# Attention and two mixture-of-experts layers on one core: row tiles of 112 and 128 partitions, a routing step and a count one block on, transposes in other PSUM banks

## The chip, the cores and the metric

The kernel runs on one core of a Trainium2 chip. The metric is device time in microseconds (us); the figure for the kernel before is the median of its timed runs. The profile is of one further execution, taken by the hardware profiler.

## The reference

Three parts follow one another, all in float32.

1. Attention as a recurrence over 768 positions, for 2 batches of 8 heads of width 48: `state = alpha * state + k v^T`, `y = q state`. The result is laid out as x with 1536 rows (tokens) of 384.
2. Layer one of experts. Each token goes to the one of 8 experts with the largest of `x @ w_gate`; an expert computes `relu(x @ w1) @ w2` (384 to 1024 to 384), weighted by the softmax's value.
3. Layer two of experts. Logits get noise scaled by `log(1 + exp(x @ w_noise))`; the best two of 8 experts are taken for each token, and their outputs, weighted by a softmax over the two, are added.

The rows of a token therefore travel: attention, one expert, then two experts, then a sum in the output.

## The kernel before, in words

**Stages.** Up to about 90 us the kernel computes attention, the first routing and the first weight splits. Then come 16 jobs in a fixed order, `jobs` (L439): layer one's experts 0 to 7 (n = 0 to 7), then layer two's (n = 8 to 15; the code calls job 8 `E`). Each job has a room of C rows: 240 in layer one; in layer two 304 for expert 0, 432 for expert 1, and for the other six, sorted by their number of rows, 432, 412, 400, 396, 384 and 384 (`CAPS`, L28). Rows travel through two stores in HBM, `xs1` and `xs2`, to which they are scattered by an indirect DMA on GpSimd's queue (`indirect`, L153) and from which the next expert loads them.

**A job.** The loop at L1131 writes out 8 hidden blocks and then 8 second blocks. A hidden block (`hidden`, L636) is nine matmuls (each operand is split into a high and a low part in the fast float32 format, hence three products for each of three slices of 384). A second block (`second`, L655) is nine more. Between the blocks the loop emits, in program order for every engine:

- `split(n + 1, q, eng)` and `split_rest()` (L498, L513): the next job's weights are cut into high and low, the high part by ScalarE (L510) and the low part by a subtraction on VectorE or GpSimd (L511), which is put off to the next `split_rest`.
- `step(prev, ...)`: one or more pieces of the job before's tail, a generator that yields between its pieces. In layer one that is `job_route2` (L788) with `route2` (L678), which computes the logits of layer two, picks two experts, ranks the rows by matmuls with a triangle of ones (L768 to L771, "the rank matmuls"), works out slots (L774 to L779), scatters the rows to `xs2` (four indirect DMAs, L780 to L782) and adds to the counts `acc2` (L784, L785; "the last piece" is L774 to L785). In layer two it is `finish2` (L836).
- `load_x`, `split_x` (L560, L584): the next job's rows are loaded and turned over.

**Where the pieces fall.** `STEPS` (L58) has three strings of 16 digits: for layer one's jobs, for job 8 and for those after. Digit i says how many pieces are done after block i (0 to 7 the hidden blocks, 8 to 15 the second ones). In the string of layer one the rank matmuls fall after second block 2 and the last piece after second block 3.

**From layer one to layer two.** Job 8 needs rows from all of layer one. `load_x(8)` is emitted in job 7 after hidden block 3 on GpSimd's queue (L1139, L566) and reads the rows that the tails of experts 0 to 5 scattered; the rows of experts 6 and 7 that go to layer two's expert 0 are put behind and handled late (`load_late`, `late_tokens`, L864 to L914). Job 7 turns x of job 8 over in second blocks 5, 6 and 7 (three PE transposes for each slice of 128, L603, then L607 on ScalarE and L608 on VectorE). In job 8 `order(2, acc2)` (L459, matmul L462) counts rows for each expert and sorts six of them; from block 3 on, the loads for job 10 use its result.

**Row tiles.** `dims` (L541) gives for each job the number of row tiles and the partitions of each. `tiles` (L552) gives the slices. In layer two a tile has 108 partitions, except in the last two jobs (128). The tiles set how rows lie in SBUF after `load_x` (row tile t, partition p is row t * p_count + p), how many rows are read, the PE transposes, and the rows of each scatter into the output.

**PSUM.** Three tags of banks: `ph` (3 buffers), `py` (3), `pm` (2) (L99 to L106). `route2` holds one `pm` buffer (`pa`) from its first piece to its last. `finish2` of job 8 is emitted by the string `AFTER` (L62) after job 8's second blocks, mixed with the late rows' work (`l`) and the turning of x for job 9 (`x`); its output transposes (L857 to L859) take `pm` buffers, and `weigh` (L824) scales a tile with ScalarE (even tiles, L827) or VectorE (odd ones, L829) and scatters it to the output.

Of the kernel before, what the change touches and what calls it, by code (L numbers as in the profile page):

```python
# [16 lines left out]
N, DM, E, F = B * S, H * D, 8, 1024  # L17
# [5 lines left out]
C2, T2 = 432, 4  # L23
# [3 lines left out]
NF2 = 2  # L27
# [27 lines left out]
LX = 9  # L55
SP = 7
WG = 8
STEPS = ("0111122111110000", "1232210200000000", "0112111010100000")  # L58
ENGS = ("VGGGGGGGGVVVVVGV", "GGGGGGGGGGGVGGVG")
XS = ("135", "024", "567")  # L60
LATE_F = 3
# [5 lines left out]
def body(tc, ap, cap, dbg=False, stop=False):  # L67
    nc = tc.nc
    V, A, G, PE = nc.vector, nc.scalar, nc.gpsimd, nc.tensor
    with ExitStack() as ctx:  # L70
# [5 lines left out]
        def sb(shape, tag, bufs, dt=F32):  # L76
            cnt[0] += 1
            return pool.tile(list(shape), dt, name=f"{tag}_{cnt[0]}", tag=tag, bufs=bufs)
# [16 lines left out]
        def ps(tag, bufs):  # L95
            cnt[0] += 1
            return psum.tile([128, 512], F32, name=f"{tag}_{cnt[0]}", tag=tag, bufs=bufs)

        def ph():  # L99
            return ps("ph", 3)  # L100
# [4 lines left out]
        def pm():  # L105
            return ps("pm", 2)  # L106
# [4 lines left out]
        xs2 = dram.tile([SPARE + 2 * E * C1 + 256, RW], F32, name="xs2")  # L111
# [86 lines left out]
        def zero_rows(store, e, n, r, k=128):  # L198

            nc.sync.dma_start(store[:E * R].rearrange("(e r) d -> r e d", e=E)[r:r + k, e:e + n],  # L200
                              zt[0][:k, None, :RW].to_broadcast([k, n, RW]))
# [9 lines left out]
        def zero_xs2():  # L211
            zero_rows(xs2, 0, 1, LOW3)
            zero_rows(xs2, 0, E, LOW2)
            zero_rows(xs2, NF2, E - NF2, C2, -C2 % 32)

        def zero_out(i):
            nc.sync.dma_start(out[i * 512:(i + 1) * 512].rearrange("(p k) d -> p (k d)", p=128), zt[0][:, :4 * DM])
# [225 lines left out]
        def place(n):  # L443

            layer, e = jobs[n]
            return e - NF2 if layer == 2 and e >= NF2 else None
# [66 lines left out]
        def split_rest():  # L513
            now, rest[:] = list(rest), []
            for o in now:
                o()
# [24 lines left out]
        def dims(n):  # L541

            layer, e = jobs[n]
            c, t = (C1, T1) if layer == 1 else (C0, T0) if e == 0 else (C2, T2)
            p = C2 // T2 if layer == 2 else c // t
            if place(n) is not None:
                c = CAPS[place(n)]
                if c <= 384:
                    t, p = 3, 128
            return t, p, c  # L550

        def tiles(n):  # L552
            nt_, p, c = dims(n)
            return [(t, slice(t * p, min(c, t * p + p)), min(c - t * p, p)) for t in range(nt_)]
# [245 lines left out]
        def tokens_of(g):  # L800

            p, t = g.shape[0], g.shape[1]
            ix, iz = sm([128, T2], "ix", I32, 3)[:p, :t], sm([128, T2], "iz")[:p, :t]
            V.tensor_scalar(iz, g[:, :, GT], 0.0, None, op0=ALU.is_equal)
            V.tensor_tensor(iz, iz, tro[:p, :t], op=ALU.mult)
            V.scalar_tensor_tensor(iz, g[:, :, TK], 0.0, iz, op0=ALU.max, op1=ALU.add)
            V.tensor_scalar(ix, iz, float(N + 128 * T2 - 1), None, op0=ALU.min)
            return ix
# [15 lines left out]
        def weigh(sc, t, y, ix, ysc, group):  # L824
            r = y.shape[0]
            if t % 2 == 0:
                A.activation(ysc[:r, t, :], y, AF.Copy, scale=sc[:r, t, :])  # L827
            else:
                V.tensor_scalar(ysc[:r, t, :], y, sc[:r, t, :], None, op0=ALU.mult)  # L829
            indirect(out, ix[:r, t:t + 1], ysc[:r, t, :], group, ALU.add)  # L830

        def by_row(n):

            return range(3) if place(n) is not None and dims(n)[2] == 384 else None

        def finish2(n):  # L836
            nt_, p, c = dims(n)
            yp = yps.pop(n)
            if by_row(n):
                ix, ysc, group = tokens_of(xg[n]), sb([p, nt_, DM], "b6", 5), []  # L840
                yield
                for t in range(nt_):
                    weigh(own[n], t, yp[t][:, :DM], ix, ysc, group)
                    yield
                return
            yT = sb([128, ND, c], "b6", 5)
            for d in range(ND):
                if d == 1:
                    V.tensor_copy(yT[:, d, :], yp[d][:, :c])
                else:  # L850
                    A.activation(yT[:, d, :], yp[d][:, :c], AF.Copy)  # L851
            ix = tokens_of(xg[n])
            ysc = sb([p, nt_, DM], "b6", 5)
            yield
            group = []
            for t, sl, r in tiles(n):
                bp = pm()  # L857
                for d in range(ND):
                    PE.transpose(bp[:r, d * 128:(d + 1) * 128], yT[:, d, sl], ident)  # L859
                weigh(own[n], t, bp[:r, :DM], ix, ysc, group)  # L860
                yield
# [261 lines left out]
        def step(it, n=1):  # L1123
            for _ in range(n if it is not None else 0):
                next(it, None)
# [5 lines left out]
        for n, (layer, e) in enumerate(jobs):  # L1131
            steps = STEPS[0 if n < E else 1 if n == E else 2]
            eng = [G if x == "G" else V for x in ENGS[layer - 1]]
            step(prev)
            for f in range(NF):
                hidden(n, f)
                split_rest()
                step(prev, int(steps[f]))
                if f == (3 if n == E - 1 else 0) and n not in (E, 2 * E - 1):  # L1139
                    load_x(n + 1, nc.gpsimd)  # L1140
                if f == 4 and layer == 2:
                    own_weight(n)
                if f % 4 == 2:
                    raw(n + 1, 2 + f // 4)
                if n != E + 1:
                    split(n + 1, f, eng[f])
                else:
                    split(n, 8 + f, eng[f])
                    if f >= 4:
                        split_rest()  # L1150
                        split(n + 1, f - 4, eng[f])
            if n < 2 * E - 1:
                for f in range(NF):
                    if n == E and f == LATE_F:
                        for _ in prev:
                            pass
                        g = load_late(nc.sync)
                        load_x(n + 1, nc.sync)
                        raw(n + 2, 0)
                        it = late_tokens(n, g)  # L1160
                    xs_ = XS[2 if n == E - 1 else layer - 1]
                    if n != E and str(f) in xs_:
                        split_x(n + 1, xs_.index(str(f)))
                    second(n, f, by_row(n))
                    split_rest()
                    step(prev, int(steps[8 + f]))
                    if n == E and f == 0:
                        order(2, acc2)
                    if f % 4 == 2 and (n, f) != (E, 2):
                        raw(n + 2, f // 4)  # L1170
                    if n < 4 and f == 5:
                        zero_out(n)
                    if n != E:
                        split(n + 1, 8 + f, eng[8 + f])
                    if n == E + 1 and f < 4:
                        split_rest()
                        split(n + 1, 4 + f, eng[8 + f])
                if n == E - NL:

                    cp = pm()  # L1180
                    PE.matmul(cp[:, 0:1], ones, acc2[:, 0:1], start=True, stop=True)
                    V.tensor_scalar(eb3[:, 0:1], cp[:, 0:1], -1.0, float(C0), op0=ALU.mult, op1=ALU.add)
                    V.tensor_scalar(eb3[:, 0:1], eb3[:, 0:1], 0.0, None, op0=ALU.max)
                prev = job_route2(n) if layer == 1 else finish2(n)
                d = 0
                for o in AFTER if n == E else ():
                    if o == "x":
                        split_x(n + 1, d)
                        d += 1
                    else:  # L1190
                        step(prev if o == "f" else it)
            else:
                nt_, p, c = dims(n)
                ix = tokens_of(xg[n])
                ysc = sb([p, nt_, DM], "b6", 5)
                group = []
                it = beyond()
                for t in range(nt_):
                    if t:
                        step(it)  # L1200
                    for f in range(NF):
                        second(n, f, (t,))
                    weigh(own[n], t, yps[n][t][:tiles(n)[t][2], :DM], ix, ysc, group)
# [217 lines left out]
```

## Time and profile before

| What | Value |
|---|---|
| Median of 3 timed runs | 482.88 us (481.26 to 483.62) |
| The profiled execution's own time | 478.29 us |
| Its span, first to last instruction | 476.7 us |
| Mean granted TensorE clock, share of 2.4 GHz | 0.996 |
| TensorE matmul busy | 460.9 us, 97% |
| VectorE, ScalarE, GpSimd busy | 318.9, 263.4, 318.9 us |
| DMA, mean over the span | 193 GB/s |

How to read it: busy time of TensorE counts pipelined matmuls, so the idle time between them is the better measure of what other engines cost it. The timeline view gives for an engine each instruction's start (us from the span's start), its duration, the engine, the line and the operation, and in square brackets how long the engine had been idle before it and what ended that. A group in it merges neighbours of one line. Line numbers are the kernel's. VectorE is DVE, ScalarE ACT, GpSimd POOL, SyncE's DMA queue SPq.

### The profile page before, as it was taken

What the parts mean: (1) busy time and instruction counts of PE and PEld (TensorE: products, weight loads), DVE (VectorE), ACT (ScalarE), POOL (GpSimd) and SP (SyncE); (2) the same over time, 40 slices, a digit from 0 to 9 for tenths busy, and PEclk for the clock granted to TensorE, in tenths of its full rate; (3) what the DMA queues carried; (4) which work ended last, traced back from release to release, by engine and by line L of the source; (5) the groups of instructions that cost most, each with busy time, mean ns of one, the idle gap of its engine ahead of it and who ended that gap; (6) DMA issues with size and microseconds to landing.
All of it is one profiled execution on the core that took longest, in us unless ns stands there. A gap on an engine that the chain in (4) does not pass through costs nothing.

```text
span 476.7 us, 9770 instructions
## 1 busy us (share of the span) xinstructions
PE 460.9 (97%) x3431; PEld 433.8 (91%) x3434; DVE 318.9 (67%) x902; ACT 263.4 (55%) x683; POOL 318.9 (67%) x400
## 2 busy tenths in 40 slices
PE   8999999999999999999899899999999999999993
PEld 4588888899999999999899799999999999999992
DVE  8999988557887887888973425935364472837440
ACT  3477787467667677676561356444553545455310
POOL 3435596576778778776865249798694958869312
PEclk9999999999999999999999999999999999999998
DMA  8984863589999978768443953778483955551232
GB/s 293 408 248 160 301 236 132 202 285 320 325 272 256 293 237 261 213 220 251 162 157 105 285 131 101 182 172 210 124 180 112 212 153 119 120 160 24 26 42 41
DMA packets 64421, 92.13 MB, mean 193 GB/s; under 512 B 22301, under 2 KB 47134, under 8 KB 64362
## 3 DMA queue, kind: packets, MB, share of 16 engines
q1 hardware_dynamic: 56202, 77.22, 53.0%
q0 software_dynamic: 8160, 14.19, 13.9%
q8 instruction: 29, 0.48, 0.4%
q14 instruction: 30, 0.25, 0.2%
HBM read 70.76 MB, written 20.63 MB: 192 GB/s over the span
## 4 chain that ended last, share of the span: by engine, by line
PE 77%; DVE 12%; issue 4%; ACT 2%; DMA 2%; POOL 2%; POOLq 0%; DVEq 0%; ACTq 0%
PE py L673 31%; PE ph L644 20%; PE ph L647 10%; DVE h L650 2%; PE pm L367 2%; PE ph L291 2%; PE pm L859 2%; DVE s L511 2%; PE pm L701 2%; PE py L338 1%; PE py L344 1%; PE py L318 1%; DVE s L238 1%; PE py L911 1%; PE ph L886 1%
## 5 line engine op out<-in xcount | busy, mean ns | idle before, releaser
L511 POOL TENSOR_TENSOR s<-s,s 128x384 fp32r<-128x384 f32 x175 | 183.1, 1231 | 38.7 <-issue 21.5
L673 PE MATMUL py<-h,s 128*128 128x240 f32 (+5 forms) x1008 | 147.3, 305 | 0.0
L673 PEld LDWEIGHTS py<-h,s 128*128 128x128 f32 x1008 | 142.6, 189 | 1.2
L644 PE MATMUL ph<-x,s 128*128 128x240 f32 (+6 forms) x768 | 135.6, 312 | 0.8 <-ACT x L630 0.6
L510 ACT ACTIVATE s<-s 128x384 fp32r<-128x384 f32 x256 | 124.7, 516 | 1.5 <-DMA s<-w 1.5
L644 PEld LDWEIGHTS ph<-x,s 128*128 128x128 f32 x768 | 115.6, 189 | 2.8 <-ACT x L630 1.0
L650 DVE SCALAR_TENSOR_TENSOR h<-ph,h 128x240 fp32r<-128x240 f32 (+6 forms) x128 | 60.8, 483 | 68.3 <-ACT h L649 67.3
L649 ACT ACTIVATE h<-ph 128x240 fp32r<-128x240 f32 (+6 forms) x128 | 55.4, 433 | 60.2 <-PE ph L647 59.9
L511 DVE TENSOR_TENSOR s<-s,s 128x384 fp32r<-128x384 f32 x81 | 79.8, 989 | 1.7 <-ACT s L510 1.4
L647 PE MATMUL ph<-x,s 128*128 128x240 f32 (+6 forms) x384 | 76.7, 308 | 0.0
L157 POOL DMA_INDIRECT out<-b,m_ix x29 | 46.6, 1607 | 37.9 <-ACT b L827 16.9
L647 PEld LDWEIGHTS ph<-x,s 128*128 128x128 f32 x384 | 61.2, 189 | 0.4
L157 POOL DMA_INDIRECT xs<-b,m_si x32 | 33.4, 1045 | 21.0 <-DVE pm L784 15.9
L300 POOL TENSOR_SCALAR_AFFINE_SELECT h<-h 128x512 f32<-128x512 f32 x24 | 22.9, 977 | 26.6 <-ACT h L299 26.6
L595 ACT ACTIVATE x<-pm 128x240 fp32r<-128x240 f32 (+5 forms) x39 | 16.9, 433 | 41.6 <-DVE pm L592 38.2
L673 PE MATMUL py<-s,h 128*128 128x384 f32 x144 | 25.9, 339 | 0.0
L673 PEld LDWEIGHTS py<-s,h 128*128 128x128 f32 x144 | 25.2, 188 | 0.0
L596 DVE TENSOR_TENSOR x<-pm,x 128x240 fp32r<-128x240 f32 (+5 forms) x39 | 18.7, 480 | 9.1 <-ACT x L595 9.1
L851 ACT ACTIVATE b<-py 128x432 f32<-128x432 f32 (+4 forms) x12 | 5.9, 501 | 27.3 <-PE py L673 27.3
L592 DVE STREAM_TRANSPOSE pm<-b 128x256 f32<-128x256 f32 (+3 forms) x39 | 20.5, 526 | 0.0
L238 DVE TENSOR_TENSOR s<-s,s 112x256 f32<-112x256 f32 (+2 forms) x24 | 19.3, 824 | 0.6
L155 POOL MEMSET spacer<- 1x1 f32 x74 | 19.6, 264 | 0.1
(244 smaller groups left out, 556.5 us busy)
## 6 DMA issues: line engine op xcount, KB each, us to landing
s<-w SPq DMA_DIRECT2D x38, 768.0 KB, 6.7
s<-w_1b SPq DMA_DIRECT2D x14, 768.0 KB, 7.3
s<-w_2b SPq DMA_DIRECT2D x12, 768.0 KB, 6.1
xs<-s SPq DMA_DIRECT2D x2, 1576.0 KB, 7.2
out<-s SPq DMA_DIRECT2D x4, 768.0 KB, 8.1
b<-xs SPq DMA_DIRECT2D x28, 96.0 KB, 5.7
b<-xs SPq DMA_DIRECT2D x12, 156.0 KB, 6.0
s<-as SPq DMA_DIRECT2D x2, 780.5 KB, 6.6
```

What stands on the lines that cost most here:

```text
L155: G.memset(spacer, 0.0)
L157: st = G.indirect_dma_start(out=dst, out_offset=bass.IndirectOffsetOnAxis(ap=ix, axis=0), in_=src, in_offset=None, **kw)
L238: eng.tensor_tensor(o, src[:, h].rearrange("r (s j) -> r s j", j=64), x[:, h].rearrange("r (s j) -> r s j", j=64), op=ALU.mult)
L300: G.affine_select(a_, a_, pattern=[[0, 4], [1, 128]], compare_op=ALU.is_ge, fill=0.0, base=0, channel_multiplier=-1)
L510: A.activation(hi[sl], t[sl], AF.Copy)
L511: rest.append(lambda: (eng or V).tensor_tensor(lo[sl], t[sl], hi[sl].bitcast(F32), op=ALU.subtract))
L592: V.transpose(y.rearrange("p (t j) -> p t j", j=32), x)
L644: PE.matmul(p, w, x[:, d, :], start=(k == 0), stop=False)
L647: PE.matmul(p, w1_of(n, f, d)[0], xl[:, d, :], start=False, stop=(d == ND - 1))
L649: A.activation(hh, p, AF.Relu)
L650: V.scalar_tensor_tensor(hl, p, 0.0, hh.bitcast(F32), op0=ALU.max, op1=ALU.subtract)
L673: PE.matmul(out_, l, r, start=(f == 0 and k == 0), stop=(f == NF - 1 and k == 2))
```

## The change

Five edits. The row tiles of layer two get 128 partitions for expert 0 (tiles of 128, 128 and 48 rows in place of 108, 108 and 88) and 112 for the others with four tiles (for 432 rows 112, 112, 112 and 96); jobs with three tiles of 128 stay. Row loads take whole tiles, so expert 0's load reads 384 rows in place of 324, and those with four tiles 448 in place of 432. The zeroing of store rows 432 to 447 takes in expert 1 as well. In layer one the rank matmuls move from after second block 2 to after block 3 and the last piece from after block 3 to after block 4. In job 8 `order` moves from after second block 0 to after block 1. The output transposes of job 8 take `ph` buffers in place of `pm`.

```diff
-STEPS = ("0111122111110000", "1232210200000000", "0112111010100000")
+STEPS = ("0111122111011000", "1232210200000000", "0112111010100000")
...
-            zero_rows(xs2, NF2, E - NF2, C2, -C2 % 32)
+            zero_rows(xs2, 1, E - 1, C2, -C2 % 32)
...
             c, t = (C1, T1) if layer == 1 else (C0, T0) if e == 0 else (C2, T2)
-            p = C2 // T2 if layer == 2 else c // t
+            p = c // t if layer == 1 else 128 if e == 0 else 112
...
             for t, sl, r in tiles(n):
-                bp = pm()
+                bp = ph() if n == E else pm()
                 for d in range(ND):
                     PE.transpose(bp[:r, d * 128:(d + 1) * 128], yT[:, d, sl], ident)
...
                     step(prev, int(steps[8 + f]))
-                    if n == E and f == 0:
+                    if n == E and f == 1:
                         order(2, acc2)
```

## Rows read from the trace of the kernel before

**Rows 1.** The page's first lines: span, busy time and share of each engine.
```profile
span 476.7 us, 9770 instructions
PE 460.9 (97%) x3431; PEld 433.8 (91%) x3434; DVE 318.9 (67%) x902; ACT 263.4 (55%) x683; POOL 318.9 (67%) x400
```

**Rows 2.** Busy time by stage: stretch and length, engines' busy, clock, DMA share, GB/s.
```profile
88.00:237.60 149.60, 147.06 (x1303) 145.44 (x1304) 120.90 (x445) 99.89 (x279) 109.07 (x140) 1.00 0.82 250
237.60:275.00 37.40, 35.24 (x237) 32.53 (x237) 18.76 (x73) 13.59 (x36) 18.42 (x25) 1.00 0.65 190
275.00:464.00 189.00, 188.96 (x1049) 185.25 (x1047) 99.98 (x178) 92.56 (x203) 139.21 (x155) 1.00 0.56 128
```

**Rows 3.** Timeline of TensorE, the instructions before which it was idle, and L886.
```profile
139.20 0.17 PE L768 MATMUL pm<-accs,tri 120*120 120x8 bf16 x1 [0.23 <-DVE m_wt L763]
...
233.12 0.45 PE L603 MATMUL pm<-iw,b 108*128 108x108 f32 x3 [1.05 <-DMA b<-xs]
...
234.99 0.45 PE L603 MATMUL pm<-iw,b 108*128 108x108 f32 x3 [0.37 <-DVE accs L785]
...
252.25 0.18 PE L462 MATMUL pm<-accs,ones 128*128 128x8 bf16 x1 [0.40 <-DVE accs L785]
...
261.52 0.52 PE L874 MATMUL pm<-iw,h 128*128 128x128 f32 x3 [0.20 <-DMA h<-xs]
...
263.09 0.54 PE L859 MATMUL pm<-iw,b 128*108 128x128 f32 x3 [0.72 <-ACT b L827]
263.38 4.40 PE L886 MATMUL ph<-s,x 128*128 128x512 f32 x18
```

**Rows 4.** The transposes' matmuls by line: duration ns min/median/max, first and last start, forms.
```profile
L603 PE MATMUL pm<-iw,b x9: 241/256/283, 233.1 to 236.5; 108*128 108x108 f32 x6, 88*128 88x88 f32 x3
...
L859 PE MATMUL pm<-iw,b x69: 270/272/318, 261.9 to 423.9; 128*108 128x128 f32 x57, 128*88 128x128 f32 x6, 128*76 128x128 f32 x3, 128*72 128x128 f32 x3
```

**Rows 5.** Timeline of VectorE around the last piece in job 6.
```profile
212.73 0.53 DVE L511 TENSOR_TENSOR s<-s,s 128x384 fp32r<-128x384 f32 x1
213.19 0.16 DVE L774 TENSOR_TENSOR pm<-pm,eb 120x16 f32<-120x16 f32 x1
...
214.25 0.17 DVE L785 CAST accs<-pm 120x8 bf16<-120x8 f32 x1
214.34 0.40 DVE L596 TENSOR_TENSOR x<-pm,x 128x240 fp32r<-128x240 f32 x1
214.65 0.55 DVE L511 TENSOR_TENSOR s<-s,s 128x384 fp32r<-128x384 f32 x1
```

**Rows 6.** Timeline of GpSimd from job 6's scatters to job 8's row load.
```profile
214.31 1.05 POOL L157 DMA_INDIRECT xs<-b,m_si  x1 [2.25 <-DVE pm L784]
...
226.04 0.87 POOL L566 DMA_DIRECT2D b<-xs  x1 [2.34 <-PE ph L647]
226.94 5.85 POOL L511 TENSOR_TENSOR s<-s,s 128x384 fp32r<-128x384 f32 x6
```

**Rows 7.** The last of job 6's four scatters, by line: duration ns, start, time to landing.
```profile
L157 POOL DMA_INDIRECT xs<-b,m_si x1: 978/978/978, 218.5 to 218.5; - x1
...
DMA to landing us min/median/max: 7.0/7.0/7.0
```

**Rows 8.** DMA queue of GpSimd between 228.9 and 232.5: packets, MB, share of 16 engines.
```profile
q0 software_dynamic: 160, 0.51, 41.3%
```

**Rows 9.** Stretches of a 108-partition row load and of weight loads; DMA share next to last.
```profile
262.00:263.00 1.00, 0.37 (x4) 0.12 (x2) 0.48 (x2) 0.92 (x2) 0.00 (x0) 1.00 0.79 295
264.00:267.00 3.00, 3.00 (x15) 2.43 (x14) 0.71 (x2) 0.39 (x1) 2.65 (x4) 1.00 1.03 360
```

**Rows 10.** Timeline of VectorE in job 7, and one more subtraction beside GpSimd's.
```profile
182.40 2.05 DVE L511 TENSOR_TENSOR s<-s,s 128x384 fp32r<-128x384 f32 x1
...
229.64 4.04 DVE L511 TENSOR_TENSOR s<-s,s 128x384 fp32r<-128x384 f32 x2
...
234.67 0.17 DVE L785 CAST accs<-pm 120x8 bf16<-120x8 f32 x1
```

**Rows 11.** ScalarE and VectorE at the end of job 8.
```profile
262.46 0.57 ACT L827 ACTIVATE b<-pm,b 108x384 f32<-108x384 f32 x1
...
262.60 0.56 DVE L877 TENSOR_TENSOR x<-pm,x 128x384 fp32r<-128x384 f32 x1 [0.52 <-ACT x L876]
```

## The prediction

> **What bounds the kernel now.** I read the page's busy shares first, then the stages, then TensorE's idle time instruction by instruction. The shares say TensorE: matmuls busy 97% of the span [rows 1]. The stages say where it is not: from 275 us to 464 us it is busy 188.96 of 189.00 us, so in layer two from job 9 on no change of loads, tiles or scatters can win time, only add some [rows 2]. In layer one (88 to 237.6) 2.54 us are idle, in job 8 (237.6 to 275) 2.16 us. The change touches both. So the prediction is a list of TensorE's waits in these two stretches, each with who ends it [rows 3]: the rank matmuls wait 0.23 us for VectorE in job 2 (and as long again in job 5; in the other layer-one jobs they don't); in job 7 the transposes of job 8's x wait 1.05 us for a DMA and, at the second slice, 0.37 us for the last piece's L785; in job 8 the count waits 0.40 us for L785, the late rows' transposes 0.20 us for their load, and the second output tile 0.72 us for ScalarE's L827.
>
> The sum is made on the profiled execution, 478.29 us (span 476.7, 1.6 around it). The median of the timed runs is 482.88, 4.6 above; I add the same difference to it.
>
> **The change, part by part.**
>
> *Row tiles, on TensorE: nothing.* L603's moving side is as wide as the tile has rows (108, 108, 88 before), and three tiles still make 304 columns; L859's is always 128 wide, for 108, 88, 76 and 72 rows alike, at a median of 272 ns [rows 4]. The counts of transposes, scatters and scalings stay. The 16 more rows of the other loads and the wider zeroing have TensorE's full stretches as cover [rows 2]; uncovered, 16 rows of 394 floats are 25 KB, 0.09 us at the 295 GB/s of a row load's stretch [rows 9].
>
> *Row tiles, on job 8's load.* It is the one row load that TensorE waits for. It is issued at 226.04, its packets run from about 228.9 to 232.5 (the queue moved 0.51 MB there) and TensorE goes on at 233.12 [rows 3, 6, 8]. It now reads 384 rows, not 324: at the old rate 3.6 us of packets become 4.3, +0.7. Against that, a 108-partition load seems not to use the whole machine: the stretch with job 9's row load shows a DMA share of 0.79, the weight loads of 128 partitions behind it 1.03 [rows 9]. With the share in proportion the packets take 4.3 x 0.79 / 1.03 = 3.3 us, -0.3. I take 0, as the queue shared the engines with weights (41.3% of 16 was its part [rows 8]), and keep -0.3 and +0.7.
>
> The Trainium skill ("DMA: Bandwidth & Descriptors", section "Why a DMA increments its semaphore by 16 and not by 1") says that a transfer is spread over the largest number up to 16 that divides its slowest dimension, so 12 engines for 108 and 16 for 112 or 128; the stretch's 0.79 agrees with 12 of 16. By it alone the packets would take 3.6 x 384/324 x 12/16 = 3.2 us, an estimate; the sum below would stay, as the wait for L785 ends last. The page also notes that some loads from GpSimd's queue use 16 anyway; no run here shows which holds.
>
> *Rank matmuls and last piece one block on.* The gain is the two waits, 2 x 0.23 = 0.46 us: a second block takes TensorE about 1 us, and L763 was only 0.23 late. The cost is in what follows the last piece. VectorE executes in program order, and the piece now stands behind one more low-part subtraction (and in jobs 1 to 6 one more x subtraction, L596). In job 6 these are the next rows: 0.40 + 0.55, so that the slots are ready 0.9 to 1.0 us later [rows 5]. GpSimd waits there (2.25 us before the first scatter [rows 6]), so four scatters move on by that, and with them whatever is queued behind them. The last of them, at 218.5, landed 7.0 us later, at 225.4; the row load issued at 226.04 reads those rows [rows 6, 7]. (The view names TensorE's L647 as releaser; its blocks come every microsecond, while the landing is the event that fits.) So the load moves on by between 0 and 0.96. Nearer 0 speaks that weight loads share the DMA and one of them, which waits for just that subtraction, now starts before the scatters; nearer 0.96, that nothing else changes. I take 0.6. The six subtractions on GpSimd (5.85 us) are queued behind that load and move with it.
>
> In job 7 itself the last piece also gets one more subtraction before it. Two took 4.04 us there while GpSimd subtracted too; alone one takes 0.55 [rows 5, 6, 10]. GpSimd's six end at 232.79, VectorE reaches the added one at 233.68: 0.55, plus some share of the 0.6 by which GpSimd is later; I take 0.3. So L785 ends 0.85 later than 234.84, and the second slice's transposes, which need its `pm` buffer, start at 235.85 instead of 234.99. The first slice's delay (0.6) is absorbed in that wait. **Cost: 0.85 us.** Bounds: -0.37 if VectorE no longer collides (that wait is then gone), +2.0 if the added subtraction collides too, at 2.05 as beside GpSimd elsewhere [rows 10].
>
> *Count one block on in job 8.* L785 is done in time then, so the 0.40 disappears at that place. But TensorE next waits for the late rows' load at 261.52, already by 0.20, and that load hangs on scatters that nothing here makes earlier: the wait there becomes 0.60 [rows 3]. Value 0, bounds 0 and -0.40. The sorted numbers come about 1.3 us later, at some 255.6; the first load that uses them stands in SyncE's queue behind the late rows' load, and the scatters before that end after 256: hidden.
>
> *Output transposes in `ph`.* The 0.72 goes: the second tile had to wait until L827 had emptied one of two `pm` banks, while `ph` has three and no hidden block is open. L886 then starts as soon as the six transposes are through, about 262.7 instead of 263.38. Its third matmul needs the low parts, ready at 263.16 [rows 11]; 18 matmuls take 4.40 us [rows 3], so two take 0.5 and there is hardly a wait. **Gain: 0.66**, bounds 0.2 (all wait for L877) and 0.72. The third tile's `ph` bank is next wanted two hidden blocks later: hidden.
>
> **Sum:** -0.46 + 0.85 + 0 - 0.66 = -0.27 us, so 478.0 for the profiled execution and 482.6 for the median. No change that can be told.
>
> **The rivals.**
>
> 1. *Forecast: the waits change places.* 482.6.
> 2. *The row load comes early.* If 16 engines and the reordered DMA traffic make it land over a microsecond sooner and VectorE's piece is no later, both waits of job 7 vanish: 0.46 + 0.72 + 1.05 + 0.37 = 2.60, 480.3. For it: the 0.79. Against it: more rows, and a scatter chain that starts later.
> 3. *A new wait in job 7 (slower).* The place is L785 ahead of the second slice's transposes; the price 2.0 us, less 1.12 of gains, is 483.8. It decides when GpSimd is still subtracting as VectorE reaches the added subtraction, which takes 0.9 us of delay of the row load (232.79 against 233.68); the scatters alone can give 0.96, the larger load 0.7 more, and then the first slice adds to it. For it: 2.05 and 4.04 in the rows [rows 10]. Against it: the earlier weight load. The Trainium skill ("SBUF — State Buffer", section "Who interferes with whom") has VectorE's operations with two SBUF inputs lock GpSimd's reads out, and the reverse, for whole instructions; the 2.05 against 0.55 agrees.
> 4. *It does not do what it says.* The rank wait turns up one block later, and L886 waits for L877: gains of 0.2 alone, cost 0.85: 483.5.
>
> **How the numbers follow.** Chances: forecast 0.50, early load 0.20, new wait 0.18, no effect 0.12. About 0.5%, 2.4 us, is what a measurement of this kernel can tell from no change. The early load is just beyond it and counts mostly as faster, with a little from the forecast's spread: 0.16. The new wait lies inside it, and passes it only if the load is late as well, or the runs scatter upward: 0.13 with a share of the last rival. The rest, 0.71, is the same. The timed runs lie within 1.2 us of their middle; the range goes from the early load, 480.3, to the new wait with that scatter, 485.0.
>
> **What would show it.** Right: no idle time before the rank matmuls in jobs 2 and 5 and before the count; the last piece in job 6 about 1 us later; the row load issued at 226.2 to 227; a wait at the second slice's transposes near 1.2 us; about 0.6 us idle before L874 and none before the second output tile. Wrong: idle time from 275 us on that wasn't there; the row load landing before TensorE asks; or a wait of over 2 us in job 7.

## The result and the profile after

The changed kernel takes 486.32 us (median of 7 runs, 485.54 to 488.01); the kernel before, timed beside it, 481.54 (481.06 to 483.62). The ratio is 1.0096, 95% interval 1.0072 to 1.012: about 1% slower, clear of the scatter of the runs, where no change was forecast. The profiled execution took 487.97, with a span of 486.4. A second set of rounds of the same kernel (e9 below) gave 1.0075 (1.004 to 1.0111).

The page of the changed kernel, span and busy time (before: [rows 1]):

```profile
span 486.4 us, 9769 instructions
PE 465.3 (96%) x3431; PEld 436.1 (90%) x3434; DVE 314.9 (65%) x902; ACT 262.0 (54%) x683; POOL 314.3 (65%) x400
```

The busy-time view by stage, in the columns of [rows 2]: jobs 6, 7 and 8, jobs 9 to 15, and what lies behind the last matmul.

```profile
203.50:222.72 19.22, 18.62 (x165) 18.19 (x163) 14.58 (x58) 12.16 (x36) 13.92 (x19) 1.00 0.67 205
222.72:244.81 22.09, 20.63 (x174) 19.43 (x173) 16.66 (x59) 13.46 (x39) 16.01 (x22) 1.00 0.76 248
244.81:281.56 36.75, 35.20 (x239) 32.52 (x237) 17.74 (x72) 13.47 (x36) 17.71 (x25) 1.00 0.63 169
281.56:474.58 193.02, 193.02 (x1074) 189.19 (x1071) 100.76 (x183) 92.75 (x203) 138.07 (x157) 1.00 0.59 127
474.58:486.37 11.79, 0.00 (x1) 0.00 (x0) 0.00 (x0) 0.58 (x1) 1.57 (x1) 0.71 0.19 27
```

The same view of the kernel before, jobs 6 to 8 and the end:

```profile
198.87:216.86 17.99, 17.99 (x164) 17.96 (x163) 15.18 (x58) 12.68 (x37) 14.28 (x19) 1.00 0.68 221
216.86:237.63 20.77, 19.36 (x173) 19.03 (x172) 18.03 (x57) 12.92 (x37) 14.38 (x21) 1.00 0.67 215
237.63:275.06 37.43, 35.27 (x239) 32.56 (x237) 18.73 (x73) 13.56 (x35) 18.39 (x25) 1.00 0.65 190
...
468.56:476.69 8.13, 0.00 (x0) 0.00 (x0) 0.00 (x0) 0.58 (x1) 1.55 (x1) 0.75 0.28 39
```

Three differences stand out: job 8 is 0.68 shorter, layer-one jobs are up to 1.3 longer, and the end of the program, with no matmul in it, is 3.66 longer. (The two profiles are 9.7 us apart, twice the difference of the medians: job 0 also starts 2.5 us later in the changed kernel's, at 93.73 in place of 91.20. That start varies with the execution: over all the kernels here it lies between 91.1 and 94.2.) The last stretch is in no row that the prediction read. The view by line says what fills it: the instructions at L1417, where the program closes, and at L1346 just ahead (duration in ns as min/median/max, then first and last start). Before:

```profile
L1417 POOLq DRAIN  x3: 46/103/1332, 474.5 to 476.4; - x3
...
L1346 POOLq INC_SWDGE_SEM  x1: 506/506/506, 474.0 to 474.0; - x1
```

After:

```profile
L1417 POOLq DRAIN  x3: 46/103/4354, 481.2 to 486.1; - x3
...
L1346 POOLq INC_SWDGE_SEM  x1: 1246/1246/1246, 479.9 to 479.9; - x1
```

Both are steps of GpSimd's sequencer (POOLq). By their place, behind the last scatter, and by what changes them below, they close GpSimd's own DMA queue, and they are called so here: the closing drain (the longest of the three DRAINs) takes 4.35 us in place of 1.33, and the step ahead of it 1.25 in place of 0.51, together 3.76 us more. The last scaling and the last scatter follow the last matmul at the same distance as before; only this is longer. The queue has hardly had more to do: 88 transfers are issued on it in either kernel, in fewer packets and with 0.6% more bytes. The DMA view gives it (packets, MB, share of 16 engines) as

```profile
q0 software_dynamic: 8160, 14.19, 13.9%
```

before, and after as

```profile
q0 software_dynamic: 7360, 14.28, 14.7%
```

TensorE's waits in the changed kernel's timeline, in the form of [rows 3]:

```profile
173.08 0.60 PE L644 MATMUL ph<-x,s 128*128 128x240 f32 x3 [0.59 <-DVE h L650]
...
241.55 0.60 PE L603 MATMUL pm<-iw,b 128*128 128x128 f32 x3 [0.87 <-DVE accs L785]
...
268.64 0.52 PE L874 MATMUL pm<-iw,h 128*128 128x128 f32 x3 [0.67 <-DMA h<-xs]
268.99 0.82 PE L859 MATMUL ph<-iw,b 128*128 128x128 f32 x6
269.74 4.54 PE L886 MATMUL ph<-s,x 128*128 128x512 f32 x18
```

The last four are the forecast's: the second slice waits 0.87 (0.37 before), the late rows 0.67 (0.20), nothing before the second output tile. The first line is new: it stands in jobs 3 to 7, waits of up to 0.6 for L650 at hidden block 5.

### The profile page after: what moved, and what is told of

The parts are those of the page before. It is cut to its first block, busy times and chain, and to the rows that moved or that the text cites. A ratio compares the mean times of both kernels' runs of the same rounds, so it can differ in the third digit from the quotient of the medians.

```text
span 486.4 us, 9769 instructions
## 1 busy us (share of the span) xinstructions
PE 465.3 (96%) x3431; PEld 436.1 (90%) x3434; DVE 314.9 (65%) x902; ACT 262.0 (54%) x683; POOL 314.3 (65%) x400
## 5 line engine op out<-in xcount | busy, mean ns | idle before, releaser
L644 PE MATMUL ph<-x,s 128*128 128x240 f32 (+6 forms) x768 | 136.8, 313 | 3.3 <-DVE h L650 2.6
L644 PEld LDWEIGHTS ph<-x,s 128*128 128x128 f32 x768 | 115.4, 189 | 6.9 <-DVE h L650 5.0
L650 DVE SCALAR_TENSOR_TENSOR h<-ph,h 128x240 fp32r<-128x240 f32 (+6 forms) x128 | 60.9, 483 | 76.3 <-ACT h L649 71.7
L649 ACT ACTIVATE h<-ph 128x240 fp32r<-128x240 f32 (+6 forms) x128 | 55.5, 434 | 67.1 <-PE ph L647 59.9
L511 DVE TENSOR_TENSOR s<-s,s 128x384 fp32r<-128x384 f32 x81 | 74.8, 929 | 1.8 <-ACT s L510 1.7
L157 POOL DMA_INDIRECT out<-b,m_ix x29 | 44.4, 1530 | 37.7 <-ACT b L827 17.0
L300 POOL TENSOR_SCALAR_AFFINE_SELECT h<-h 128x512 f32<-128x512 f32 x24 | 21.7, 927 | 30.7 <-ACT h L299 30.1
L595 ACT ACTIVATE x<-pm 128x240 fp32r<-128x240 f32 (+5 forms) x39 | 16.9, 433 | 40.4 <-DVE pm L592 31.5
L596 DVE TENSOR_TENSOR x<-pm,x 128x240 fp32r<-128x240 f32 (+5 forms) x39 | 18.8, 482 | 8.9 <-ACT x L595 8.9
```

What stands on the lines that cost most here:

```text
L157: st = G.indirect_dma_start(out=dst, out_offset=bass.IndirectOffsetOnAxis(ap=ix, axis=0), in_=src, in_offset=None, **kw)
L300: G.affine_select(a_, a_, pattern=[[0, 4], [1, 128]], compare_op=ALU.is_ge, fill=0.0, base=0, channel_multiplier=-1)
L511: rest.append(lambda: (eng or V).tensor_tensor(lo[sl], t[sl], hi[sl].bitcast(F32), op=ALU.subtract))
L644: PE.matmul(p, w, x[:, d, :], start=(k == 0), stop=False)
L649: A.activation(hh, p, AF.Relu)
L650: V.scalar_tensor_tensor(hl, p, 0.0, hh.bitcast(F32), op0=ALU.max, op1=ALU.subtract)
```

## The experiments

Every ratio is to the kernel before, timed in the same rounds on the same chip. Its medians there were 480.19 (e1 to e4), 479.29 (e5 to e8) and 480.07 (e9 to e12).

**First guess: the later scatters.** The waits for L650 in jobs 3 to 7 begin with ScalarE's relu L649 of hidden blocks 0 and 1, up to 2.5 us behind its matmuls, and beside it run the four scatters, which the change moved on. Four kernels took the steps apart. e1, the changed kernel with

```diff
-STEPS = ("0111122111011000", ...
+STEPS = ("0111122111110000", ...
```

> The changed kernel with the old places of the routing steps; row tiles, count and output transposes stay changed. Theory A (the whole loss comes from the last routing piece, whose four scatters now run beside the next job's first hidden blocks): the waits of L644 for L650 are gone in jobs 3 to 7, and what the other edits gain in job 8 is left, about 0.7 us: ratio 0.998 to 1.000 to the kernel before. Theory B (the row tiles of 112 and 128 rows, their zeroing and their loads lose the time): the loss stays, ratio 1.007 to 1.012. Theory C (the loss is in the count or the output transposes of job 8): the loss stays too, and stands in job 8.

Measured: 482.88, ratio 1.0063 (1.0024 to 1.0101). Without the new steps the loss is mostly still there, so theory A is not its main part. Jobs 2 to 6 take as long as before (90.86 us against 90.79), job 8 is 36.84, and the end is 12.10 us long.

e2, the kernel before with the new steps alone:

> The kernel before with the new places of the routing steps and nothing else. Theory A: TensorE waits at hidden block 5 of jobs 3 to 7 as in the changed kernel, jobs 3, 4, 6 and 7 are each 1.1 to 1.3 us longer than before, ratio 1.008 to 1.013 (the 0.7 us gained in job 8 is missing). Theories B and C: ratio 0.999 to 1.002, with the rank waits of jobs 2 and 5 gone.

Measured: 480.77, ratio 1.0018 (0.9976 to 1.0061), with the scatters 1.0 to 1.6 us later, counted from the next job's first matmul, and no wait for L650 in jobs 3 to 7. Theory A has fallen as the main cause.

e3, the kernel before with "0111122111020000", and e4, with "0111122111101000":

> The kernel before with the rank matmuls one block on and the last piece (low-part VectorE work, four scatters) where it was, in the same block as the rank matmuls but after them. Theory A: scatters start at most a few tenths of a us later, no wait of L644 for L650, the rank waits of jobs 2 and 5 gone: ratio 0.998 to 1.001. Rival D (it is the rank matmuls' place that disturbs the next job): the waits at hidden block 5 stay, ratio 1.007 to 1.012. A third way: VectorE now waits for the rank matmuls just issued, so the scatters are as late as in the changed kernel, and the loss stays by theory A's own mechanism; then the first scatter starts about 1 us later than before.

> The kernel before with only the last routing piece one block on; the rank matmuls stay. Theory A: first scatter about 1 us later, L644 waits for L650 in jobs 3 to 7, ratio 1.008 to 1.013, and the rank waits of 0.23 us in jobs 2 and 5 are still there. Rival D: no loss, ratio 0.999 to 1.002.

Measured: e3 478.88, ratio 0.9974 (0.9937 to 1.001); e4 482.06, ratio 1.0041 (1.0003 to 1.0079), with a rank wait of 0.23 to 0.25 us in each of jobs 3 to 6, which take 18.6 to 18.8 us each for some 18.1. In e3 the row load of job 8 goes out earlier:

```profile
224.52 0.87 POOL L566 DMA_DIRECT2D b<-xs  x1 [0.92 <-PE ph L647]
```

That is 7.8 us after job 7's first matmul, where [rows 6] have 9.2. VectorE's two colliding subtractions take 2.56 in place of 4.04 [rows 10], and job 7 is 19.37 us long, not 20.77. Jobs 2 to 6 gain nothing there (90.79), so all of it is won in job 7; why the load can go earlier was not followed further. Moving half of what the change moved was the better place in this profile; e3's interval still includes 1.

**Second guess: the row tiles, and the end.** e5 is the kernel before with both row-tile lines of the diff; e6 has 128 for expert 0 alone, e7 112 for the others alone (with the wider zeroing); e8 is the changed kernel with the old tiles and the old zeroing. The row-tile line of the first three:

```diff
-            p = C2 // T2 if layer == 2 else c // t
+            p = c // t if layer == 1 else 128 if e == 0 else 112   # e5
+            p = c // t if layer == 1 else 128 if e == 0 else 108   # e6
+            p = c // t if layer == 1 else 108 if e == 0 else 112   # e7
```

> The kernel before with only the row tiles of 128 and 112 (and the zeroing that goes with them). Theory E (the row tiles lengthen the end of the program: after the last transfer has landed, GpSimd's closing drain of its own queue takes 4.35 us in place of 1.33 and the step before it 1.25 in place of 0.51): everything up to the last matmul is as before within 0.5 us, the stretch after it 11.8 to 12.1 us in place of 8.1, ratio 1.006 to 1.009. Rival F (that end belongs to the count's or the output transposes' new place): the end stays at 8.1 us, ratio 0.998 to 1.002.

> The kernel before with tiles of 128 rows for the first expert of the second layer alone; the others stay at 108. It tells which loads lengthen the end. If it is the one wide load: closing drain 4.35 us, ratio 1.006 to 1.009. If it goes with the number of loads: a seventh or less of the 3.7 us, ratio 1.000 to 1.002. If it is the 112-row tiles alone: drain 1.33 as before, ratio 0.999 to 1.001.

> The kernel before with tiles of 112 rows for the experts of the second layer that had 108, with the zeroing; the first expert stays at 108. If the 112-row tiles lengthen the end: closing drain 4.35 us, step before it 1.25, ratio 1.006 to 1.009. If only the 128-row load does: drain 1.33, ratio 0.999 to 1.001.

> The changed kernel with the old row tiles (324 and 432 rows, 108 partitions) and the old zeroing; steps, count and output transposes stay changed. Theory E: the stretch after the last matmul is back at 8.1 us, 3.7 shorter than in the changed kernel, and job 8 keeps its gain of 0.7; the ratio to the kernel before is 0.999 to 1.003. Theory A in what is left of it (late scatters delay the relu of the next job's first hidden blocks, by execution rather than always): waits of L644 for L650 in some of the jobs 3 to 7, and then a ratio up to 1.005. Rival F: ratio 1.007 to 1.012 as in the changed kernel.

Measured: e5 482.87, 1.0066 (1.004 to 1.0092); e6 479.85, 1.0021 (0.9995 to 1.0047); e7 482.76, 1.0068 (1.0041 to 1.0094); e8 479.02, 0.9995 (0.9975 to 1.0016). The closing lines of e7:

```profile
L1417 POOLq DRAIN  x3: 46/103/4395, 478.2 to 483.1; - x3
...
L1346 POOLq INC_SWDGE_SEM  x1: 1256/1256/1256, 476.9 to 476.9; - x1
```

and of e6:

```profile
L1417 POOLq DRAIN  x3: 46/103/1251, 475.8 to 477.6; - x3
...
L1346 POOLq INC_SWDGE_SEM  x1: 486/486/486, 475.2 to 475.2; - x1
```

So the tiles of 112 rows are the cause: they alone bring the loss, and taking the tiles back removes it. (The wider zeroing went with them each time. It is issued on SyncE's queue, not on the one that closes, but was not taken out by itself.) Bytes are not what the drain goes by: e7 moved the 14.19 MB of the kernel before on this queue and drained 4.40 us, e6 14.29 MB and 1.25. The durations don't depend on the execution: 4.354 in the changed kernel, e1, e5 and e9 alike, and 1.332 in the kernel before, e2, e3, e4, e8 and e12.

**Why a queue that moved fewer packets closes more slowly.** The guess was a count with a turn, so that what is left to clear depends on where the count stands at the end. Small transfers were put on GpSimd's queue, one in each of jobs 9 to 14:

```diff
+                if f == 6 and 9 <= n <= 14:
+                    G.dma_start(scr[:, 64 * (n - 9):64 * (n - 8)].rearrange("p (k w) -> p k w", w=16)[:, :, :8],
+                                ident[:, :32].rearrange("p (k w) -> p k w", w=8))
```

e9 is the changed kernel again, e10 the changed kernel with these six, e11 the kernel before with them.

> The changed kernel once more, to be compared in the same rounds and to see which of its losses recur. Theory E: the closing drain is 4.35 us and the end 11.8 us again. If the late relus of the next job's first hidden blocks belong to the kernel, jobs 3, 4, 6 and 7 are again 1.1 to 1.3 us longer than before and the ratio is 1.009 to 1.012; if they belong to one execution, those jobs are as before and the ratio is 1.005 to 1.008 (3.7 us of closing drain less about 0.7 gained).

> The changed kernel with six more small transfers on GpSimd's queue (128 partitions of 4 pieces of 32 bytes, one in each of jobs 9 to 14, to a scratch tensor nobody reads). Theory H (the closing drain goes with where the count of the queue's descriptors stands when the program ends, and jumps where that count passes a full turn): the drain falls from 4.35 us to between 1.2 and 2.5, the step before it from 1.25 to about 0.5 to 0.9, and the kernel is faster than the changed one by 2 to 3.5 us: ratio to the kernel before 0.998 to 1.003. Rival I (the drain is long because the loads of 112 rows use more DMA engines, or goes up with the work on the queue): the drain is 4.35 or longer, ratio 1.006 to 1.012.

> The kernel before with the same six transfers. Theory H: it has just passed the turn, so the same addition that shortens the changed kernel's drain lengthens this one's, from 1.33 to between 1.7 and 2.6 us: ratio 1.000 to 1.003. Rival I: as for the changed kernel, the drain stays at 1.33 or rises by what six transfers out of some ninety are worth, 0.1 us.

Measured: e9 483.89, 1.0075 (1.004 to 1.0111); e10 480.79, 1.002 (0.9989 to 1.0051); e11 481.82, 1.0042 (1.002 to 1.0063). The same addition shortened one drain and lengthened the other. e10:

```profile
L1421 POOLq DRAIN  x3: 46/103/1904, 475.1 to 477.6; - x3
```

e11:

```profile
L1421 POOLq DRAIN  x3: 46/103/2231, 477.9 to 480.7; - x3
```

e13 to e15 are the changed kernel with one, two and four of the transfers, e16 the kernel before with twelve; one profiled execution each (485.23, 485.07, 481.91 and 486.14 us, the kernel before beside them 482.79).

> The changed kernel with one of the six small transfers, in job 9. If the closing drain is a ramp with one jump (0.15 us for each such transfer, from the 0.90 that six added to the kernel before; down by 3.3 to 3.6 at the jump), the changed kernel at 4.35 stands near the top of the ramp. This one either still climbs, 4.50 us, or has passed the jump, 1.15.

> The changed kernel with two of the six transfers, in jobs 9 and 10. Ramp with a jump: most likely past it, closing drain 1.30 us, end after the last matmul about 8.1; if the jump lies further on, 4.65. If the drain falls in proportion to the added transfers instead (a third of the way from 4.35 to 1.90): 3.5.

> The changed kernel with four of the six transfers, in jobs 9 to 12. Ramp with a jump: closing drain 1.60 us (1.90 less two times 0.15). Fall in proportion: 2.7.

> The kernel before with twelve such transfers, two in each of jobs 9 to 14. Ramp: closing drain 3.13 us (1.33 and twelve times 0.15), the step before it about 0.95, and the end after the last matmul about 10.6 us. If the drain only depends on which side of a bound the count is: 2.2 as with six.

Measured, with two and with four transfers:

```profile
L1421 POOLq DRAIN  x3: 46/103/4599, 478.0 to 483.2; - x3
```

```profile
L1421 POOLq DRAIN  x3: 46/103/1659, 477.8 to 480.0; - x3
```

All of them, in us:

| kernel | step before the drain | closing drain | last matmul to end of span |
|---|---|---|---|
| before | 0.51 | 1.33 | 8.13 |
| before + 6 (e11) | 0.73 | 2.23 | 9.37 |
| before + 12 (e16) | 0.89 | 2.88 | 10.10 |
| changed | 1.25 | 4.35 | 11.79 |
| changed + 1 (e13) | 1.28 | 4.48 | 11.96 |
| changed + 2 (e14) | 1.31 | 4.60 | 12.07 |
| changed + 4 (e15) | 0.59 | 1.66 | 8.66 |
| changed + 6 (e10) | 0.65 | 1.90 | 8.97 |

It is a ramp with a jump. Each transfer adds 0.11 to 0.15 us on either side, and between two and four the drain falls by 2.94. The step ahead and the drain go together: in every kernel of this document 0.01 us of the step stands for 0.041 of the drain, as if both counted the same thing. It shows in the timed runs: e10 is 3.1 us faster than e9 in the same rounds, and its two closing steps are 3.05 shorter. The program closes at L1421 in these kernels, as they have four lines more. The jump came one or two transfers later than I thought likeliest for e14, and the ramp with twelve is flatter than the 3.13 I expected. What the queue counts, and over how many the count runs, no run here shows. It isn't the number of transfers alone, which is 88 before and after, and a single count with one fixed turn doesn't fit either: the jump takes 2.94 and two transfers' 0.24 off, some 3.2 us, so with a turn above 4.60 no drain could be shorter than 1.4, yet 1.33 (before) and 1.25 (e6) occur.

**A version that beats both.** e12 is the kernel before with the rank matmuls alone moved ("0111122111020000"), `order` at f == 1 and the output transposes in `ph`:

> The kernel before with the parts of the change that gained by themselves: the rank matmuls one block on with the last piece where it was, the count one block on, the output transposes of the one expert in the other banks; the row tiles stay at 108. No rank wait in jobs 2 and 5, no wait before the second output tile, job 8 about 0.6 us shorter, closing drain 1.33: 1 to 2 us faster than before, ratio 0.995 to 0.999. If the count's new place only moves the wait to the late rows, 0.4 us less of that.

Measured: 478.70, ratio 0.9974 (0.9956 to 0.9993). Job 7 is 19.67, job 8 36.81, the end 8.05. It is faster than the kernel before by about 1.3 us, its interval just clear of 1. The gains in jobs 7 and 8 add up to 1.7; job 10 is 31.29 here against 29.82 in the profile of before.

**What the tiles of 112 rows win in job 10.** That loss goes with the tiles. In the nine kernels with tiles of 112 rows job 10 takes 29.52 to 29.55 us, in the nine with 108 it takes 29.77 to 32.52, six of them over 31. VectorE makes one subtraction late in job 9 beside a row of them on GpSimd; it lasts 8.61 us in e8 (108 rows) and 5.91 in e9 (the changed tiles and zeroing, otherwise the same kernel), and in e8 TensorE then waits in job 10, whose x VectorE and ScalarE (L595) finish turning only behind it:

```profile
294.47 8.61 DVE L511 TENSOR_TENSOR s<-s,s 128x384 fp32r<-128x384 f32 x1 [0.69 <-ACT s L510]
...
304.26 0.66 PE L644 MATMUL ph<-x,s 128*128 128x432 f32 x2 [0.63 <-ACT x L595]
...
310.65 1.44 PE L644 MATMUL ph<-x,s 128*128 128x432 f32 x6 [0.94 <-DVE h L650]
```

and in e9 it doesn't:

```profile
298.51 5.91 DVE L511 TENSOR_TENSOR s<-s,s 128x384 fp32r<-128x384 f32 x1 [0.69 <-ACT s L510]
```

GpSimd's row of subtractions starts later in e8, behind the second scatter of job 9, which goes out 8.33 us after the job's first matmul against 5.94 in e9; why the scatter is later with 108 rows was not followed. So the change brings a gain of 0.2 to 3 us in job 10 along with the loss at the end. The rank matmuls alone, tiles of 112 and a few more transfers in one kernel were not tried.

**What remains of the first guess.** Lengths of stretches between the first L644 of a job and that of a later one, in us:

| steps | kernels | jobs 2 to 6 | job 7 |
|---|---|---|---|
| old | before, e1, e5, e6, e7, e11 | 90.79 to 90.86 | 20.36 to 21.51 |
| new | e2, e8, e9, e10 | 90.17 to 90.48 | 20.62 to 24.32 |
| old | e16 | 93.70 | 20.44 |
| new | changed, e13, e14, e15 | 92.91 to 94.09 | 21.62 to 22.09 |

Relus of hidden blocks 0 and 1 over 0.3 us late are in the kernels of the last two lines and in no other of these jobs 2 to 7, under either steps. Four of those five kernels (e13 to e16) were profiled together on one chip, on which none of e1 to e12 ran, so the chip may be part of it (that of the changed kernel's profile is not on record). The new steps are not needed for it: e16 runs the code of the kernel before up to job 8. In job 4 of e16, TensorE ends hidden block 0 at 164.46 + 0.51:

```profile
163.79 0.84 PE L644 MATMUL ph<-x,s 128*128 128x240 f32 x6
164.46 0.51 PE L647 MATMUL ph<-x,s 128*128 128x240 f32 x3
```

and ScalarE starts its relu two microseconds later, after two stretches of idling:

```profile
165.57 0.37 ACT L795 ACTIVATE b<-py 128x240 f32<-128x240 f32 x1 [1.06 <-PE ph L647]
167.02 0.37 ACT L649 ACTIVATE h<-ph 128x240 fp32r<-128x240 f32 x1 [1.08 <-PE pm L701]
```

In the changed kernel's profile it looks the same at block 1 of job 4 (the relu at 170.34, its matmuls done at 167.82); in e9, the same program, that relu follows at once. So most of the 3.3 us that jobs 2 to 6 lose between the two profiles belongs to the occasion, not to the change. What delays the relus there stays open.

## Why the prediction was wrong

- **Row tiles, "on TensorE: nothing": the step that failed.** For TensorE nothing was lost: job 9 to the last matmul takes 193.02 us against 193.50. But the sum was made of TensorE's waits alone, and the tiles act behind the last matmul. "No change of loads, tiles or scatters can win time, only add some" warned of a loss, but no row of the stretch behind 468.56 was then read; and its first half was wrong, by at least 0.2 us in job 10. Measured: +3.0 us on the closing drain, +0.74 on the step ahead of it. With that term the forecast of -0.27 becomes +3.5. On the forecast's base of 482.88 that is 486.4, close to the measured 486.32 by luck: the kernel before itself was 481.54 over all its runs, and the difference to explain is 4.8. The forecast's sign of being wrong, idle time from 275 us on, did come, but behind the last matmul.
- **Row tiles, job 8's load.** Taken as 0 with -0.3 and +0.7. From its issue to the first transposes that need it, e5 (old steps, new tiles) takes 233.49 - 227.08 = 6.41 us, with the wait still there, against 7.08 before [rows 3, 6], with 60 rows more:

```profile
227.08 0.83 POOL L566 DMA_DIRECT2D b<-xs  x1 [2.52 <-PE ph L647]
...
233.49 0.60 PE L603 MATMUL pm<-iw,b 128*128 128x128 f32 x3 [0.57 <-DMA b<-xs]
```

  By the rule of the Trainium skill ("DMA: Bandwidth & Descriptors", section "Why a DMA increments its semaphore by 16 and not by 1") 108 partitions go to 12 engines and 128 to 16, and 3.6 us of packets become an estimated 3.2; the trace agrees in the sign, -0.67. Over all kernels in which TensorE still waits for this load the time is 6.2 to 6.7 us with 128 partitions and 6.6 to 7.7 with 108. As forecast it brought nothing: e5's second slice then waits 0.68 for L785.
- **Rank waits, -0.46: right.** Gone in jobs 2 and 5; in the kernels with the new steps and without late relus jobs 2 to 6 are 0.3 to 0.7 shorter.
- **Last piece in job 7, +0.85: right in kind, its size not shown.** L785 became the wait that ends last, but the forecast delay of the row load by 0.6 did not come: counted from job 7's first matmul it goes out at 9.45 in the changed kernel, 9.17 in e2 and 8.52 in e8, against 9.18 before, though the scatters moved on by 1.0 to 1.6 where 0.9 to 1.0 was forecast. Over the eight kernels with the new steps job 7 averages 22.09 against 20.94 over the seven with the old ones, +1.15. But four of the eight have late relus and two (22.86 and 24.32) a cost of another kind, below; the two with neither, e8 and e10, average 21.19, 0.2 above the six old ones without late relus, and TensorE's two waits there sum to 1.35 and 1.52, for 1.42 before. Rival 3, a wait of over 2 us in job 7, did not come: the longest with the new steps is 1.35.
- **Count, 0: right.** Its wait went to the late rows, 0.20 to 0.67.
- **Output transposes, -0.66: right.** L886 starts 0.75 after L859; job 8 is 0.57 to 0.75 shorter than before in the changed kernel, e1, e8, e10 and e12; in e9 the slower clock reaches into it.
- **Rival 2, the early row load: right about its worth, wrong about its cause.** The earlier load and the shorter collision came with the rank matmuls alone (e3, e12), not with the load on 128 partitions: job 7 is then 1.1 to 1.4 us shorter.

The sum is then +3.76 - 0.5 + 1.15 - 0.65 = +3.8 us with job 7's average, +2.8 with the 0.2 of the undisturbed kernels, less what job 10 wins, 0.3 against the profile of before. Measured were 4.8 (486.32 - 481.54) and, in e9's rounds, 3.8. So the closing steps are the main part, shown by e5 to e8; the rest of the timed difference is of the size of what comes and goes with the occasion, and is not told apart term by term.

## What to carry to other kernels

The path to the end does not stop at the last matmul: read the stretch behind it instruction by instruction, the sequencers' closing steps too, before a change of transfers is costed at nothing. Where a GpSimd DMA queue is used, its closing drain is part of the time, and its length is no measure of the work: here fewer packets made it three times as long, so after any change of tile shape or transfer count look at it, and try a few transfers more if it landed high. When a step and what follows it move together, try moving each alone: here one half won in its profile, the other lost. And before a difference between two kernels is put down to chance, sort all the runs by each edit: job 10's looked like chance until the tiles were put beside it.

## What the runs showed of the hardware that was not expected

GpSimd's closing drain goes up by 0.11 to 0.15 us for each small transfer on its queue and falls, between two and four of them, from 4.60 to 1.66 us; the step ahead of it falls with it, from 1.31 to 0.59.

In job 7 of e9 two waits cost more than their sum. TensorE waits 0.61 and, 2.7 us on, 0.89; the busy-time view (columns as in [rows 2]) then shows the granted clock at 0.50, the lower level of 1.2 GHz, until about 242, and in e2 the job shows the same for 3.4 us:

```profile
234.00:236.00 2.00, 1.11 (x7) 0.62 (x5) 1.81 (x8) 0.06 (x1) 0.97 (x1) 0.79 0.24 36
236.00:238.00 2.00, 2.00 (x9) 1.91 (x10) 0.94 (x2) 0.83 (x2) 1.57 (x5) 0.50 1.08 401
238.00:240.00 2.00, 2.00 (x9) 1.58 (x9) 0.39 (x1) 0.83 (x2) 1.75 (x4) 0.50 0.73 229
240.00:242.00 2.00, 2.00 (x11) 2.00 (x10) 0.49 (x2) 0.74 (x2) 0.95 (x1) 0.50 0.39 114
242.00:244.00 2.00, 2.00 (x17) 2.00 (x16) 0.57 (x2) 0.42 (x1) 0.00 (x0) 1.00 0.87 229
```

Nine to eleven matmuls fall in 2 us there in place of 17, and the job is 24.32 us long; in e10, the same code up to there, the two waits sum to as much (0.17 and 1.35), the clock stays at 1.00, and the job takes 21.76. The kernel before, with waits of 1.05 and 0.37 at the same places, and e7, with 0.79 and 0.85, kept 1.00 too. On some occasions, under old steps and new, ScalarE's relu starts up to 2.5 us after the matmuls it waits for; the runs don't show why.
